# Paired PSUM banks, joined copies and sums, deferred activations and other attention places in a sketched attention and SwiGLU kernel

## The chip, the cores and the metric

The kernel runs on one core of a Trainium2 chip. The metric is the device time of one execution in microseconds; several executions are taken, and their median counts. Profiles are of one execution and give the span from the first to the last instruction.

## The reference

Four images (batches) of 1088 tokens with four heads of 32 go through a polynomial-sketch attention without softmax, and its output, 4352 tokens of 128, through a SwiGLU block with 1536 hidden channels. All is computed in float32.

```python
def phi(x):                                    # r = 8, so 64 features
    a = np.einsum('rd,bhsd->bhsr', S1, x)
    b = np.einsum('rd,bhsd->bhsr', S2, x)
    return np.einsum('bhsi,bhsj->bhsij', a, b).reshape(*x.shape[:-1], r * r)
q_p, k_p = (phi(q), phi(k))
kv = np.einsum('bhsf,bhsd->bhfd', k_p, v)
z = np.sum(k_p, axis=2)
num = np.einsum('bhsf,bhfd->bhsd', q_p, kv)
den = np.einsum('bhsf,bhf->bhs', q_p, z)[..., None] + 1e-06
attn = num / den
x = attn.transpose(0, 2, 1, 3).reshape(B * S, H * D)
g = x @ w_gate
out = (g * (1 / (1 + np.exp(-g))) * (x @ w_val)) @ w_out
```

## The kernel before

The tokens of each image are cut into three blocks of 384, 384 and 320 (`blocks`, numbers 0 to 11), the hidden channels into 12 chunks of 128. A unit is one block with one chunk: it makes the gate product and the value product of 128 channels by 384 or 320 tokens, the activation, and their product, the hidden tile. `down` then multiplies one hidden tile by 128 rows of `w_out` and adds it up in a PSUM bank over the 12 chunks of a block; after the twelfth, `store` transposes the bank on VectorE (DVE) and sends it out.

The program's order is the schedule: the engines work off their own queues in the order in which the code issues the instructions.

The first image's three blocks are worked in `unit` with whole float32 products, interleaved with the attention of images 0 and 1. From block 3 on a loop over y from 0 to 107 (units in the order of `line`) does the rest; the prediction numbers its units by y. There `cut_unit` makes a product out of three faster passes in place of one float32 product. Weights and tokens are split ahead of time into a high part, a scaled low part and a difference (`cut_weights`, `cut_tokens`: w1, wb, wd and x1, x0, xd). A first pass makes d = wd times xd, and two passes make p = w1 x1 + wb x0. ScalarE (ACT) copies d with a scale (L890), DVE adds p (L893), ACT takes the activation (L897) and GpSimd (POOL) multiplies activation and value to the hidden tile (L902). Up to y = 21 only the value product is made this way and the gate is a float32 product (L880); from y = 22 (`GATES`) both are. The gate's weights are split on the way, in rows of four steps each from y = 0, 1, 5 and 5 on (`gate_rows`, on ACT and DVE, L849).

PSUM has eight banks. Bank 3 holds the sums of `down` (`acc`). `bank()` hands out the one of the others that was touched longest ago; `wide("a")` is banks 4 and 5, `wide("b")` 6 and 7, which the attention uses. A unit with both products takes four single banks.

The attention of images 1 to 3 is a generator, `attentions()`. Each `yield` ends a part; the loop asks for parts (`parts_of`) after a unit: after each one up to y = 21, after every second one later. Large groups of TensorE work are marked `yield "pe"` and are placed before units 6, 8, 22, 24 and 40 (`GROUPS`). The first group of image b has the products of values and key features (`values`, L370), of the key sums (L698) and, for image 2, the key products of the next image (L336). `fold` and `spread_out` then take the results on DVE. The second has the query products (L324); the third, `numerators` (L760), ends in copies to `xT`. The key sums are five additions on POOL (`feature_sums`, L529); `beside` issues one of them with each part of the transpositions that follow. `query_step` begins with a chain of small DVE operations for the denominators (L727 to L733).

`todo` lists finished units; after each unit, one `down` is issued (two at times) when more than five are listed, or six where a new block begins.

Of the kernel before, what the change touches and what calls it, by code (L numbers as in the profile page):

```python
# [7 lines left out]
FP32 = mybir.dt.float32  # L8
# [4 lines left out]
AF = mybir.ActivationFunctionType  # L13
# [6 lines left out]
def kernel(  # L20
# [89 lines left out]
    def bank(tag=None):  # L110

        if tag is not None:
            i = place[tag]
        elif oldest[0]:
            i = min((i for i in used if i not in held), key=used.get)
        else:
            i = place[free_banks[turn[0] % len(free_banks)]]
            turn[0] += 1
        touch(i)
        return PS[:, i, :]  # L120

    def wide(tag):
        i = place[tag]
# [473 lines left out]
    def attentions():  # L597

        yield from turn_keys(1)
        yield from turn_queries(1)
        hold("a")
        kp = wide("a")
        for i, c in enumerate(kpieces):
            key_products(kp[:, i, :], *c)
        ka = apool.tile([P, NC * H, R], FP32, tag="kas", name="kas")

        def sketch(ps, i):
            c0, c1 = kpieces[i]  # L610
# [36 lines left out]

        phk = apool.tile([P, NC, H, R, R], FP32, tag="phk", name="phk")
        yield from features(phk, kab)
        zs, sums = feature_sums(phk)  # L650
        yield from beside(turn_keys(3), sums)
        yield from beside(turn_queries(2), sums)
        for b in (2, 3):
            yield "pe"
            if b == 3:
                numerators(2, spread)
            hold("a")
            kv = bank()
            release("a")
            values(kv, phk, zs)  # L660
            if b == 2:
                kab, copies = sketched(wide("a"), key_products, 2, "kab2")
                run_copies(copies, 2)
            fold(kv)
            spread = spread_out(b, kv)
            yield
            yield "pe"
            qab, copies = sketched(wide("b"), query_sketches, 3, "qab")
            run_copies(copies, 2)
            yield  # L670
# [112 lines left out]
    acc = {}  # L783
# [67 lines left out]
    def cut_tokens(i, engine=nc.gpsimd):  # L851
# [14 lines left out]
            op0=ALU.mult, op1=ALU.add,  # L866
        )

    def cut_unit(i, j, both=False):

        t0, n = blocks[i]
        x1, x0, xd = (x[:, 0:n] for x in x_parts[i])
        ws = (wg, wv) if both else (wv,)
        parts = [[x[:, j % 3, :] for x in w_parts[id(w), j // 3]] for w in ws]
        ds = [bank()[:, 0:n] for _ in ws]
        g = None if both else bank()[:, 0:n]
        for d, (_, _, wd) in zip(ds, parts):
            nc.tensor.matmul(d, wd, xd, start=True, stop=True)  # L878
        if not both:
            nc.tensor.matmul(g, wg[:, j, :], xT[:, t0 : t0 + n], start=True, stop=True)  # L880
        ps = []
        for w1, wb, _ in parts:
            p = bank()[:, 0:n]
            nc.tensor.matmul(p, w1, x1, start=True, stop=False)  # L884
            nc.tensor.matmul(p, wb, x0, start=False, stop=True)  # L885
            ps.append(p)
        sums = []
        for d in ds:
            s = fpool.tile([P, BW], FP32, tag="sgl", name="sum", bufs=6)[:, 0:n]
            nc.scalar.activation(s, d, AF.Copy, scale=-1.0 / BETA)  # L890
            sums.append(s)
        for p, s in zip(ps, sums):
            nc.vector.scalar_tensor_tensor(  # L893
                out=s, in0=p, scalar=1.0 + 1.0 / BETA, in1=s, op0=ALU.mult, op1=ALU.add
            )
        sg = fpool.tile([P, BW], FP32, tag="sg", name="sg", bufs=5)[:, 0:n]
        nc.scalar.activation(sg, sums[0] if both else g, AF.Silu)  # L897
        slot_of[i, j] = slots.pop(0)
        hj = hbuf[:, slot_of[i, j], :]
        hidden[i, j] = hj  # L900
        todo.append((i, j))
        nc.gpsimd.tensor_tensor(out=hj[:, 0:n], in0=sg, in1=sums[-1], op=ALU.mult)  # L902

    def unit(i, j, late=False, between=(None, None)):


        t0, n = blocks[i]
        g, u = bank(), bank()
        for o, w in ((g, wg), (u, wv)):
            if between[0] and w is wv:  # L910
                between[0]()
            nc.tensor.matmul(  # L912
                o[:, 0:n], w[:, j, :], xT[:, t0 : t0 + n], start=True, stop=True
            )
        sg = fpool.tile(
            [P, BW], FP32, tag="sgl" if late else "sg", name="sg", bufs=6 if late else 5
        )
# [14 lines left out]

    def catch_up():
        o, sg = lates.pop(0)
        nc.gpsimd.tensor_tensor(out=o, in0=o, in1=sg, op=ALU.mult)

    def down():

        i, j = todo.pop(0)
        n = SPLIT if i == LAST else blocks[i][1]  # L940
        if j == 0:
            acc[i] = bank("g1" if i == 1 else "acc")
        nc.tensor.matmul(  # L943
            acc[i][:, 0:n],
            wo[:, j, :],
# [199 lines left out]
    for z, (i, j) in enumerate(seq):  # L1145
# [16 lines left out]
        if z == 20:  # L1162
            lows = [
                pool.tile([P, 3, P], FP32, tag=tag, name="low", bufs=bufs)[:]
                for pool, tag, bufs in ((apool, "qb", 2), (apool, "dT", 2), (apool, "rd", 2), (fpool, "sgl", 6))
            ]
            first, low, second, third = cut_weights(wv, lows, nc.gpsimd)
        if z in (20, 21):
# [27 lines left out]

    line = [3 * b + k for b in range(1, B) for k in ((0, 2, 1) if b == B - 1 else range(3))]
    END = len(line) * NCH  # L1200
    GROUPS, GATES = (6, 8, 22, 24, 40), 22

    token_steps = {}
    for m, i in enumerate(line[1:], 1):
# [7 lines left out]
    for y in range(END):  # L1212
        i, j = line[y // NCH], y % NCH
        if y in GROUPS:
            group()
        if y == END - 1:
            unit(i, j)
        else:
            cut_unit(i, j, both=y >= GATES)
        for _ in range(2):  # L1220

            if len(todo) > min(5 + (todo[0][1] == 0), END - y + 1):
                down()
        parts_of(y < GATES or y % 2 == 0)
        if y == 0:
            gate_rows = cut_weights(wg, lows, nc.vector)
        for n, row in enumerate(gate_rows):
            if y >= (0, 1, 5, 5)[n]:
                take(row, 1)
        for gen in token_steps.get(y, ()):  # L1230
            next(gen, None)
# [43 lines left out]
```

## Time and profile before

| | us |
|---|---|
| median of 8 runs | 293.37 |
| lowest and highest | 291.91, 295.06 |
| the profiled execution | 293.55 |
| its span | 291.7 |
| loop over y, from its first product | 93.15 |
| last product of the loop's last unit ends about | 283.7 |

The mean granted TensorE clock is 0.994. The operations that the change touches, from the table of groups by shape (108 to 283 us):

| line, engine | columns | mean ns |
|---|---|---|
| L890 ACT copy of d | 384 / 320 | 485 / 430 |
| L893 DVE sum with p | 384 / 320 | 551 / 485 |
| L897 ACT activation of a sum | 384 / 320 | 526 / 472 |
| L902 POOL product | 384 / 320 | 1064 / 926 |

A float32 product stands in the trace as two matrix instructions, a pass of parts as one. The ends of matrix instructions are modelled, and one that waits for the engine before it shows a longer time; so starts are the safer numbers. The idle time that a row gives is that of its engine, and it costs something only where the engine is the one that sets the end.

### The profile page before, as it was taken

What the parts mean: (1) busy time and instruction counts of PE and PEld (TensorE: products, weight loads), DVE (VectorE), ACT (ScalarE), POOL (GpSimd) and SP (SyncE); (2) the same over time, 40 slices, a digit from 0 to 9 for tenths busy, and PEclk for the clock granted to TensorE, in tenths of its full rate; (3) what the DMA queues carried; (4) which work ended last, traced back from release to release, by engine and by line L of the source; (5) the groups of instructions that cost most, each with busy time, mean ns of one, the idle gap of its engine ahead of it and who ended that gap; (6) DMA issues with size and microseconds to landing.
All of it is one profiled execution on the core that took longest, in us unless ns stands there. A gap on an engine that the chain in (4) does not pass through costs nothing.

```text
span 291.7 us, 6382 instructions
## 1 busy us (share of the span) xinstructions
PE 282.4 (97%) x2307; PEld 213.7 (73%) x2307; DVE 206.5 (71%) x422; ACT 181.4 (62%) x432; POOL 162.6 (56%) x183
## 2 busy tenths in 40 slices
PE   8899999999999969999999999999999999999995
PEld 6545566656656657777787778888888988888984
DVE  3997988874667954999668876656767676676651
ACT  3467565732303826555467677788788887888860
POOL 3315322389301784589737666557666675766650
PEclk9999999999999979999999999999999999999999
DMA  7564293312410213001001001001001010010101
GB/s 193 153 215 110 58 288 100 104 51 83 108 21 15 52 57 88 0 1 27 7 12 27 2 0 24 2 0 31 0 0 27 2 24 1 2 27 0 23 2 27
DMA packets 26142, 14.33 MB, mean 49 GB/s; under 512 B 19840, under 2 KB 24192, under 8 KB 26112
## 3 DMA queue, kind: packets, MB, share of 16 engines
q1 hardware_dynamic: 25456, 13.84, 18.6%
q8 instruction: 18, 0.29, 0.4%
q10 hardware_dynamic: 656, 0.10, 0.2%
q14 instruction: 12, 0.10, 0.1%
HBM read 11.41 MB, written 2.23 MB: 47 GB/s over the span
## 4 chain that ended last, share of the span: by engine, by line
PE 86%; DVE 5%; POOL 3%; ACT 3%; issue 2%; DMA 2%; SPq 0%; DVEq 0%; POOLq 0%; ACTq 0%
PE PS L943 26%; PE PS L912 15%; PE PS L878 10%; PE PS L884 10%; PE PS L885 10%; PE PS L880 4%; PE PS L336 2%; PE PS L324 2%; PE PS L760 2%; POOL zs L529 2%; DMA kld<-in_k_dram 2%; ACT sum L890 1%; PE PS L370 1%; POOL hbuf L902 1%; DVE sum L893 1%
## 5 line engine op out<-in xcount | busy, mean ns | idle before, releaser
L902 POOL TENSOR_TENSOR hbuf<-sg,sum 128x384 f32<-128x384 f32 (+1 forms) x107 | 109.3, 1023 | 62.9 <-ACT sg L897 51.2
L893 DVE SCALAR_TENSOR_TENSOR sum<-PS,sum 128x384 f32<-128x384 f32 (+1 forms) x192 | 93.9, 526 | 50.2 <-ACT sum L890 42.1
L943 PE MATMUL PS<-hbuf,wo 128*128 128x384 f32 (+2 forms) x288 | 103.0, 459 | 0.0
L890 ACT ACTIVATE sum<-PS 128x384 f32<-128x384 f32 (+1 forms) x192 | 80.3, 464 | 13.5 <-PE PS L878 13.2
L897 ACT ACTIVATE sg<-sum 128x384 f32<-128x384 f32 (+1 forms) x85 | 42.7, 503 | 27.4 <-DVE sum L893 27.4
L943 PEld LDWEIGHTS PS<-hbuf,wo 128*128 128x128 f32 x288 | 52.0, 189 | 10.3 <-issue 0.4
L878 PE MATMUL PS<-xd,gphq 128*128 128x384 f32 (+1 forms) x85 | 47.9, 564 | 0.0
L884 PE MATMUL PS<-x,w 128*128 128x384 f32 (+1 forms) x107 | 42.2, 394 | 0.1
L878 PE MATMUL PS<-xd,wd 128*128 128x384 f32 (+1 forms) x107 | 39.7, 371 | 0.7 <-DVE sum L893 0.4
L885 PE MATMUL PS<-x,wb 128*128 128x384 f32 (+1 forms) x107 | 35.0, 327 | 0.0
L918 ACT ACTIVATE sg<-PS 128x384 f32<-128x384 f32 (+1 forms) x37 | 17.4, 473 | 22.0 <-PE PS L912 20.3
L912 PE MATMUL PS<-xT,wg 128*128 128x384 f32 (+1 forms) x74 | 29.5, 480 | 0.0
L912 PE MATMUL PS<-xT,wv 128*128 128x384 f32 (+1 forms) x74 | 28.8, 471 | 0.2 <-DVE wv L270 0.2
L878 PEld LDWEIGHTS PS<-xd,wd 128*128 128x128 f32 x107 | 20.4, 190 | 11.5 <-DVE sum L893 1.2
L884 PE MATMUL PS<-x,graw 128*128 128x384 f32 (+1 forms) x85 | 27.9, 328 | 0.0
L885 PE MATMUL PS<-x,graw 128*128 128x384 f32 (+1 forms) x85 | 27.6, 325 | 0.0
L929 DVE TENSOR_TENSOR hbuf<-sg,PS 128x384 f32<-128x384 f32 (+1 forms) x31 | 16.2, 526 | 10.8 <-PE PS L912 10.5
L884 PEld LDWEIGHTS PS<-x,w 128*128 128x128 f32 x107 | 20.1, 188 | 4.2 <-ACT sum L890 0.5
L878 PEld LDWEIGHTS PS<-xd,gphq 128*128 128x128 f32 x85 | 16.1, 189 | 8.6 <-issue 0.4
L885 PEld LDWEIGHTS PS<-x,wb 128*128 128x128 f32 x107 | 20.2, 188 | 2.9
L912 PEld LDWEIGHTS PS<-xT,wv 128*128 128x128 f32 x74 | 13.8, 190 | 9.2 <-DVE hbuf L929 0.9
L912 PEld LDWEIGHTS PS<-xT,wg 128*128 128x128 f32 x74 | 13.3, 189 | 9.3 <-issue 1.2
(130 smaller groups left out, 347.5 us busy)
## 6 DMA issues: line engine op xcount, KB each, us to landing
kld<-in_k_dram SPq DMA_DIRECT2D x4, 544.0 KB, 4.4
vld<-in_v_dram SPq DMA_DIRECT2D x12, 144.0 KB, 5.2
qld<-in_q_dram SPq DMA_DIRECT2D x3, 544.0 KB, 3.4
raw<-in_moe_w_out_dram SPq DMA_DIRECT2D x4, 384.0 KB, 4.6
out_dram<-o SPq DMA_DIRECT2D x28, 48.0 KB, 1.9
raw<-in_moe_w_gate_dram SPq DMA_DIRECT2D x3, 384.0 KB, 3.2
raw<-in_moe_w_val_dram SPq DMA_DIRECT2D x3, 384.0 KB, 3.3
out_dram<-o SPq DMA_DIRECT2D x16, 40.0 KB, 1.7
```

Of the source, the lines that this page charges most:

```text
L878: nc.tensor.matmul(d, wd, xd, start=True, stop=True)
L880: nc.tensor.matmul(g, wg[:, j, :], xT[:, t0 : t0 + n], start=True, stop=True)
L884: nc.tensor.matmul(p, w1, x1, start=True, stop=False)
L885: nc.tensor.matmul(p, wb, x0, start=False, stop=True)
L890: nc.scalar.activation(s, d, AF.Copy, scale=-1.0 / BETA)
L893: nc.vector.scalar_tensor_tensor(out=s, in0=p, scalar=1.0 + 1.0 / BETA, in1=s, op0=ALU.mult, op1=ALU.add)
L897: nc.scalar.activation(sg, sums[0] if both else g, AF.Silu)
L902: nc.gpsimd.tensor_tensor(out=hj[:, 0:n], in0=sg, in1=sums[-1], op=ALU.mult)
L912: nc.tensor.matmul(o[:, 0:n], w[:, j, :], xT[:, t0 : t0 + n], start=True, stop=True)
L918: nc.scalar.activation(sg[:, 0:n], g[:, 0:n], AF.Silu)
L929: nc.vector.tensor_tensor(out=hj[:, 0:n], in0=sg[:, 0:n], in1=u[:, 0:n], op=ALU.mult)
L943: nc.tensor.matmul(acc[i][:, 0:n], wo[:, j, :], hidden[i, j][:, 0:n], start=(j == 0), stop=(j == NCH - 1),)
```

## The change

What it does:

- The five key sums of image 2 are issued together, before the transpositions of the next keys and queries.
- A unit with both products takes two pairs of neighbouring banks (`pair`, out of banks 0-1, 4-5 and 6-7) in place of four single ones: one for both d, one for both p. ACT copies both d in one instruction of twice the size, and DVE makes both sums in one.
- In such a unit the activation and the POOL product are put off (`ending`) and issued by `finish` in the next unit, behind that unit's copy. The unit is listed for `down` then.
- Both products are made of parts from y = 26 on, and before that at y = 11, 14, 17, 20 and 23.
- The groups stand before y = 5, 7, 26, 28 and 52. Parts of the attention are asked for after each unit up to y = 7, after two of three up to 25, and after every third one from there.
- The rows of gate weights begin at y = 0, 2, 6 and 6.
- `acc` is bank 2 for every second block from block 5 on, and bank 2 is held back from y = 26. The rule with six listed units is left for one block alone.
- The buffers of the sums are four of two halves instead of six single ones; the fourth low part of the value weights has another home.

```diff
+    def pair():
+        i = min((i for i in (0, 4, 6) if i not in held), key=lambda i: max(used[i], used[i + 1]))
+        touch(i, i + 1)
+        return PS[:, i : i + 2, :]
...
         zs, sums = feature_sums(phk)
-        yield from beside(turn_keys(3), sums)
-        yield from beside(turn_queries(2), sums)
+        for f in sums:
+            f()
+        yield from turn_keys(3)
+        yield from turn_queries(2)
...
             kv = bank()
+            kv_bank = [max(used, key=used.get)]
...
             spread = spread_out(b, kv)
+            touch(*kv_bank)
...
+    room = [None, 2]
+    def doubles(k):
+        if room[1] + k > 2:
+            room[:] = fpool.tile([P, 2, BW], FP32, tag="sgl", name="sum", bufs=4), 0
+        at = room[1]
+        room[1] += k
+        return room[0][:, at : at + k, :]
...
-        ds = [bank()[:, 0:n] for _ in ws]
+        ds = pair()[:, :, 0:n] if both else bank()[:, 0:n].unsqueeze(1)
         g = None if both else bank()[:, 0:n]
...
-        ps = []
-        for w1, wb, _ in parts:
-            p = bank()[:, 0:n]
...
-        for d in ds:
-            s = fpool.tile([P, BW], FP32, tag="sgl", name="sum", bufs=6)[:, 0:n]
-            nc.scalar.activation(s, d, AF.Copy, scale=-1.0 / BETA)
...
-        for p, s in zip(ps, sums):
-            nc.vector.scalar_tensor_tensor(
-                out=s, in0=p, scalar=1.0 + 1.0 / BETA, in1=s, op0=ALU.mult, op1=ALU.add
-            )
...
+        sums = doubles(len(ws))[:, :, 0:n]
+        nc.scalar.activation(sums, ds, AF.Copy, scale=-1.0 / BETA)
+        finish()
+        ps = pair()[:, :, 0:n] if both else bank()[:, 0:n].unsqueeze(1)
+        for k, (w1, wb, _) in enumerate(parts):
+            nc.tensor.matmul(ps[:, k], w1, x1, start=True, stop=False)
+            nc.tensor.matmul(ps[:, k], wb, x0, start=False, stop=True)
+        nc.vector.scalar_tensor_tensor(
+            out=sums, in0=ps, scalar=1.0 + 1.0 / BETA, in1=sums, op0=ALU.mult, op1=ALU.add
+        )
+        def last():
+            sg = fpool.tile([P, BW], FP32, tag="sg", name="sg", bufs=5)[:, 0:n]
+            nc.scalar.activation(sg, sums[:, 0] if both else g, AF.Silu)
...
+            todo.append((i, j))
+            nc.gpsimd.tensor_tensor(out=hj[:, 0:n], in0=sg, in1=sums[:, len(ws) - 1], op=ALU.mult)
+        if both:
+            ending.append(last)
+        else:
+            last()
...
+    ending = []
+    def finish():
+        while ending:
+            ending.pop(0)()
...
-            acc[i] = bank("g1" if i == 1 else "acc")
+            acc[i] = bank("g1" if i == 1 else "g2" if i in line[2::2] else "acc")
...
-                for pool, tag, bufs in ((apool, "qb", 2), (apool, "dT", 2), (apool, "rd", 2), (fpool, "sgl", 6))
+                for pool, tag, bufs in ((apool, "qb", 2), (apool, "dT", 2), (apool, "rd", 2), (apool, "qb", 2))
...
-    GROUPS, GATES = (6, 8, 22, 24, 40), 22
+    GROUPS, GATES = (5, 7, 26, 28, 52), 26
...
+        if y == GATES:
+            hold("g2")
         if y == END - 1:
+            finish()
             unit(i, j)
         else:
-            cut_unit(i, j, both=y >= GATES)
+            cut_unit(i, j, both=y >= GATES or (y > 10 and y % 3 == 2))
         for _ in range(2):
-            if len(todo) > min(5 + (todo[0][1] == 0), END - y + 1):
+            if len(todo) > min(5 + (todo[0] == (line[1], 0)), END - y + 1):
                 down()
-        parts_of(y < GATES or y % 2 == 0)
+        parts_of(y < 8 or (y % 3 != 2 if y < GATES else y % 3 == 0))
...
-            if y >= (0, 1, 5, 5)[n]:
+            if y >= (0, 2, 6, 6)[n]:
                 take(row, 1)
```

More of the change, by code (lines that the diff above doesn't have):

```diff
@@ L874, in cut_unit @@
         parts = [[x[:, j % 3, :] for x in w_parts[id(w), j // 3]] for w in ws]
-        ds = [bank()[:, 0:n] for _ in ws]
+        ds = pair()[:, :, 0:n] if both else bank()[:, 0:n].unsqueeze(1)
         g = None if both else bank()[:, 0:n]
-        for d, (_, _, wd) in zip(ds, parts):
-            nc.tensor.matmul(d, wd, xd, start=True, stop=True)
+        for k, (_, _, wd) in enumerate(parts):
+            nc.tensor.matmul(ds[:, k], wd, xd, start=True, stop=True)
         if not both:
             nc.tensor.matmul(g, wg[:, j, :], xT[:, t0 : t0 + n], start=True, stop=True)
-        ps = []
@@ L882, in cut_unit @@
-        for w1, wb, _ in parts:
-            p = bank()[:, 0:n]
[L884 to L887, printed above, removed]
-        for d in ds:
-            s = fpool.tile([P, BW], FP32, tag="sgl", name="sum", bufs=6)[:, 0:n]
-            nc.scalar.activation(s, d, AF.Copy, scale=-1.0 / BETA)
-            sums.append(s)
-        for p, s in zip(ps, sums):
-            nc.vector.scalar_tensor_tensor(
-                out=s, in0=p, scalar=1.0 + 1.0 / BETA, in1=s, op0=ALU.mult, op1=ALU.add
-            )
@@ L896, in cut_unit @@
[L896 to L902, printed above, removed]
+        sums = doubles(len(ws))[:, :, 0:n]
+        nc.scalar.activation(sums, ds, AF.Copy, scale=-1.0 / BETA)
+        finish()
+        ps = pair()[:, :, 0:n] if both else bank()[:, 0:n].unsqueeze(1)
@@ new lines, in cut_unit @@
+        for k, (w1, wb, _) in enumerate(parts):
[7 more added lines that the diff above has]
+            nc.scalar.activation(sg, sums[:, 0] if both else g, AF.Silu)
+            slot_of[i, j] = slots.pop(0)
+            hj = hbuf[:, slot_of[i, j], :]
+            hidden[i, j] = hj
+            todo.append((i, j))
+            nc.gpsimd.tensor_tensor(out=hj[:, 0:n], in0=sg, in1=sums[:, len(ws) - 1], op=ALU.mult)
@@ L914, in unit @@
             )
-        sg = fpool.tile(
-            [P, BW], FP32, tag="sgl" if late else "sg", name="sg", bufs=6 if late else 5
-        )
+        sg = doubles(1)[:, 0, :] if late else fpool.tile([P, BW], FP32, tag="sg", name="sg", bufs=5)
         nc.scalar.activation(sg[:, 0:n], g[:, 0:n], AF.Silu)
@@ L935, in catch_up @@
         nc.gpsimd.tensor_tensor(out=o, in0=o, in1=sg, op=ALU.mult)
+    line = [3 * b + k for b in range(1, B) for k in ((0, 2, 1) if b == B - 1 else range(3))]
     def down():
@@ L1195 @@
     slots[:] = range(NH - 10)
-    line = [3 * b + k for b in range(1, B) for k in ((0, 2, 1) if b == B - 1 else range(3))]
     END = len(line) * NCH
-    GROUPS, GATES = (6, 8, 22, 24, 40), 22
+    GROUPS, GATES = (5, 7, 26, 28, 52), 26
     token_steps = {}
```

## The prediction

> **What bounds the kernel now.** I read the busy shares first, then the table of stretches, then the chain of waits between 96 and 110 us, then single queues.
>
> ```profile
> PE 282.4 (97%) x2307; PEld 213.7 (73%) x2307; DVE 206.5 (71%) x422; ACT 181.4 (62%) x432; POOL 162.6 (56%) x183
> ...
> 100.00:104.50 4.50, 2.19 (x77) 1.51 (x75) 4.50 (x8) 1.40 (x3) 4.42 (x5) 0.99 0.39 124
> 104.50:108.60 4.10, 4.08 (x49) 3.52 (x50) 1.27 (x5) 1.32 (x4) 4.10 (x4) 0.60 0.06 12
> ...
> 147.00:157.50 10.50, 10.39 (x64) 8.27 (x54) 7.92 (x18) 7.43 (x20) 5.68 (x7) 1.00 0.02 4
> 157.50:173.00 15.50, 15.36 (x78) 12.48 (x76) 13.08 (x26) 10.70 (x28) 9.44 (x10) 1.00 0.09 14
> 181.00:284.00 103.00, 103.00 (x523) 89.11 (x522) 66.92 (x140) 83.77 (x198) 66.46 (x69) 1.00 0.06 10
> ```
>
> In the stretches the columns are length, then busy PE, weight load, DVE, ACT, POOL, granted clock, DMA. From 181 to 284 us TensorE is never idle. Busy is not proof of peak, so I took the spacing of starts: unit after unit (six passes of 0.173 us and one output product of 0.646 us, sum 1.69) the output product starts at 239.76, 241.45, 243.14: 1.69 us apart. That stage has no slack; only TensorE work counts there. The hole is at 100 to 108.6: TensorE is idle for 2.3 us and then runs at a mean clock of 0.60.
>
> ```profile
> 96.41 0.97 POOL hbuf L902
> ...
> 97.39 1.28 POOL zs L529
> 98.67 0.94 POOL hbuf L902
> ...
> 99.91 1.28 POOL zs L529
> 101.19 1.28 POOL hbuf L902
> 102.47 1.00 POOL zs L529
> ...
> 103.55 0.93 POOL zs L529
> ...
> 104.52 0.44 PE PS L698 x8
> 104.97 2.12 PE PS L336 x36
> ```
>
> This chain (start, length, what) ends last there: the five key sums of image 2 stand on POOL between gate products (L902), because `beside` hands one out per step. The value product L698 waits for the last of them. After the wait the key products take 2.12 us; the same 36 took 1.20 at 57.01 and at 69.33. What the hole costs, from starts on TensorE: unit 5 waits 0.55 (99.06 to 99.61, for a bank that the sum of unit 2 on DVE frees); L698 waits 2.3, with 0.25 around it; the key products are 0.9 too long; unit 6 is 0.5 too long. Sum 4.5 us. The gaps from 139 to 177 us, as spacing above 0.173, 0.147, 0.646 or 0.54, come to about 3.7: 0.4 in the groups up to 147, 2.0 in gaps of 0.1 to 0.4 until 173, 1.3 around the last attention group at 173.35.
>
> **What the Trainium skill says.** "TensorE: Matmul & The Clock Gate", section "What's actually happening": after an idle window of about 3.4 us the matrix clock drops to half until it has been busy as long. The trace agrees in kind: 0.60 behind the hole, near 1.00 elsewhere; the hole itself is only 2.3 us, in a stretch that is half idle. "SBUF — State Buffer", section "SBUF: two separate sides": a DVE operation with two SBUF inputs and a GpSimd operation that reads SBUF exclude each other for the whole instruction. The trace fits it: the same 128x384 difference (L849 on DVE) takes 1.08, 1.50, 0.90 and 0.61 us beside POOL work. "Perfetto Trace Analysis", section "Optimizing Scalar/DVE Operations": each instruction carries a fixed access cost, so larger ones amortise it, but breaking up may help where a large one causes bubbles elsewhere. The rows agree on the fixed part: DVE's L893 takes 551 ns on 384 columns and 485 on 320, ACT's L890 485 and 430.
>
> **Part by part.**
>
> *Key sums in one go.* In the changed order all five sums stand ahead of the first gate product. First sum 92.70 to 94.13; the second waits for the last feature block (DVE, 94.68); then 1.28, 1.28, 1.03, 0.92: done at 99.2. The group moves from unit 6 to unit 5, so unit 4 (ends 99.06) is followed by the value products: 1.2 us, then L698 at 100.3. The sums are a microsecond early. The first bank of the group needs DVE's sum of unit 2, which now stands before the first weight difference, not behind it (gate rows begin at unit 2): transposes 0.8, 0.7, 0.8 and three sums of 0.5 from 95.03 end at 98.6. The key products need the bank of unit 3's sum for their second half, at 101.2; DVE has it at 101.0 if one difference takes 1.1, at 101.4 if 1.5. Key products 100.5 to 101.7, units 5 and 6 with one output product each to 105.3. The query group then wants the fold: differences at 1.0 each put it at 103.5 and its result at 104.3; with three of 1.5, nothing excludes that, at 106. So after these units and two output products TensorE stands at 105.3, where before it stood at 109.94 (unit 7's true start). Gain 4.6; bounds 3.3 (all three differences 1.5, waits of 0.2 and 0.9 put in) and 4.7. With no hole the clock stays up; that is in these numbers. Delayed gate products: unit 0's moves from 96.41 to 99.2, but its first reader is an output product at about 102.9. I take 4.3.
>
> *Units with both products in parts.* Before, units 22 to 106: 85. After, 26 to 106 and 11, 14, 17, 20, 23: 86. One more exchange of 0.646 for three passes of 0.173: gain 0.13.
>
> *Joined copies and sums.* By the two sizes, ACT's copy costs 155 ns plus 0.86 a column: joined 0.82 for 2x384 and 0.71 for 2x320, in place of 0.97 and 0.86. DVE's sum is 155 plus 1.03: 0.95 and 0.81. 86 units save some 13 us on each engine, but beside TensorE at its peak this is worth nothing by itself. The price is a later first result. Worst case, 320-wide unit of 1.42 us (0.88 plus a 320 output product): both ds products end at 0.29, copy 0.5 to 1.2 (0.2 from product to copy, as 240.58 to 240.78), sum 1.25 to 2.07. Three pairs rotate: ds of unit y+2 takes the pair of unit y's sum at 2.83 (slack 0.76); ps of unit y+1 takes the pair of unit y's copy at 1.71 (slack 0.5). The activation of unit y now stands behind copy y+1, so ACT no longer waits for DVE first; its result is read by an output product six units later instead of five. ACT load 0.71+0.47 of 1.42. So nothing is added as long as DVE is free.
>
> *DVE not free.* In units 26 to 52 attention parts come every third unit, each near 1.0 us: sum y+1 then ends at 3.9 of 4.25, no wait. The chain of denominators (148.90 to 150.94, 2.04 us) stands behind sum 30: sum 31 ends at 4.95, ds of unit 33 wanted it at 4.25: wait 0.7. At the group of unit 26 no output product lies between unit 26 and 27, because the deferred unit adds nothing to the list; unit 27's pair holds bank 1, which fold and transposition read for 1.0 us after the value products (142.04 to 143.41 before, 1.4): wait 0.4 to 0.9. The query group needs the pair of sum 27: wait 0.5. One copy behind the query copies: 0.2. Sum about 2.0; against 2.4 before (0.4 + 2.0). At unit 52 the numerators need sum 51 (0.6) and unit 52's second pair the copy out of bank 4 (0.7): 1.3, as before. Bounds: none of these waits but the last, gain 2.4, to twice them, loss 1.6. I take a gain of 0.4.
>
> *Mixed stage, units 11 to 25.* Three units take 5.3 us (units 1.17, 1.17, 1.04, three output products); DVE has two sums of 0.55, one of 0.95 and two parts near 1.0. The chain of denominators at unit 15 delays sum 17 to 7.6 us after its start; its bank is wanted at 7.8. I take 0; up to 1 if it slips.
>
> *Output banks.* Alternating banks 2 and 3 remove the extra unit of delay at a block change; the trace shows no wait there (two products together at 237.58 and 256.71). 0. The fourth weight tile moves to another buffer, read last at 28 us: 0.
>
> *End.* One more output product is left behind the last line (1.2 us of its products, 0.86, behind it instead of 1.7), so the last transposition, its DMAs and those of the last copy lie closer together: plus 0.2; 0 to 0.6.
>
> Sum: -4.3 - 0.1 - 0.4 + 0.2 = -4.6. The profiled execution took 293.55 (span 291.7 and 1.85 around it): 288.95. It lies 0.2 above the median of 293.37, so I forecast 288.9.
>
> **Rivals.** 0.5% is 1.5 us, about what a measurement of this kernel tells from no change.
> - *Likeliest, 0.55*: as summed, 287.4 to 290.4.
> - *The waits of units 26 to 52 go as well, 0.12*: 4.6 + (2.4 - 0.4) = 6.6, so 286.9. For it: DVE is busy only 7.9 of 10.5 us there. Against: the chain of denominators is one block of 2 us.
> - *DVE takes POOL's place in the hole, 0.15*: differences of 1.5 against back-to-back gate products, the fold late, and half clock again: gain 3.3, less 0.9 for the clock, less the other lines at nothing: about 291. For it: 1.50 at 100.10. Against: two others took 0.9 and 0.61.
> - *The pairs bind, slower, 0.12*: three pairs where single banks freed half by half. It decides once the way from ds to the end of the sum passes 2.83 us in a 320 unit (2.07 by my count), or copy plus reach passes 1.71. A two-bank access dearer by 0.45 on each of ACT and DVE does that; then each of some 81 units loses about 0.1, 8 us, less 4.3: 297. Against: two-bank copies of xT take 589 (ACT, 512 columns) and 692 ns (DVE), no dearer than one-bank rates.
> - *Gain and new waits cancel, 0.06*: 293.
>
> Faster by over 0.5%: 0.55 + 0.12 + 0.13 = 0.80; within 0.08; slower 0.12. The range 286.5 to 292.3 holds all but the slower cases and a few per cent.
>
> **What would show it.** Right: the five sums adjoin on POOL from 92.7 to about 99.3, L698 starts near 100.3 without a wait on POOL, the key products take 1.2, the clock stays near 1.00 from 100 to 110; the joined sums take about 0.95 and 0.81. Wrong in the middle: more than 1 us of waits on DVE's sum at units 33 or 27. Wrong in the large: unit spacing in the last 100 us above 1.69 (384) or 1.42 (320), then the pairs bind.

## The result

| kernel | median us (range) | ratio to before [95%] | span of the profiled execution |
|---|---|---|---|
| before | 293.38 (291.85 to 295.06, 31 runs) | | 291.7 |
| after | 289.76 (289.38 to 290.98, 11 runs) | 0.9887 [0.9865, 0.9909] | 288.3 |

The gain is 3.6 us at the median; the forecast was 288.9, a gain of 4.5. Part of that gain is the end of a loss of clock that the kernel before has only in some of its executions, described in the last section: 12 of the 31 took 291.85 to 292.50 us, the other 19 took 293.23 or more, and against the median of the 12 (292.09) the gain is 2.3 us. The start of the program is not the same in all profiles, so what follows it is compared on a clock of its own: "the loop" below runs from the first product of unit 0 with `xd` to the end of the span. It took 198.6 us before and 194.9 after: 3.7 less.

The profile after, first the busy shares on its page:

```profile
PE 279.2 (97%) x2308; PEld 212.2 (74%) x2308; DVE 205.8 (71%) x337; ACT 173.4 (60%) x347; POOL 162.5 (56%) x183
```

DVE and ACT issue 85 instructions fewer each, the joined sums and copies. TensorE's busy time fell by 3.2 us, though it has the same products but for one exchange; 1.4 us of that, by the prediction's reading, is what key products and a unit had lost at half clock. Next the stretches (columns as in the prediction):

```profile
100.00:104.50 4.50, 4.50 (x103) 3.66 (x91) 4.43 (x10) 2.21 (x6) 4.50 (x5) 1.00 0.39 124
104.50:108.60 4.10, 4.10 (x82) 3.02 (x81) 2.29 (x4) 2.58 (x7) 4.10 (x4) 1.00 0.11 22
...
155.00:171.00 16.00, 14.71 (x78) 12.65 (x77) 13.95 (x18) 11.65 (x21) 9.23 (x11) 1.00 0.07 11
180.00:280.00 100.00, 99.75 (x559) 84.73 (x558) 63.24 (x73) 73.62 (x130) 62.97 (x67) 1.00 0.06 10
```

The hole of 100 to 108.6 us is closed: TensorE is busy throughout, at a mean clock of 1.00 where it was 0.60. The last hundred microseconds are nearly as full as before (99.75 of 100 against 100.00; the rest is one wait of 0.24 at unit 52), and the output products there start 1.69 us apart as before (173.43, 175.12, 176.81). A new hole stands between 155 and 171 us: 1.3 us in which TensorE is idle, against 0.25 in that stretch before.

POOL's queue at the key sums (start, length, engine, line, operation; in brackets the idle time ahead and what ended it):

```profile
92.98 1.43 POOL L535 TENSOR_TENSOR zs<-phk 128x512 f32<-128x512 f32 x1 [14.15 <-DVE phk L365]
95.03 1.28 POOL L535 TENSOR_TENSOR zs<-phk 128x512 f32<-128x512 f32 x1 [0.63 <-DVE phk L365]
96.40 2.11 POOL L535 TENSOR_TENSOR zs<-zs 128x512 f32<-128x512 f32 x2
98.59 0.74 POOL L535 TENSOR_TENSOR zs<-zs,phk 128x256 f32<-128x256 f32 x1
99.28 4.85 POOL L919 TENSOR_TENSOR hbuf<-sg,sum 128x384 f32<-128x384 f32 x4
```

And TensorE's own queue there:

```profile
99.42 1.21 PE L376 MATMUL PS<-phk,vld 128*32 128x64 f32 x72
100.45 0.29 PE L708 MATMUL PS<-zs,ones 128*32 128x64 f32 x8
100.68 1.27 PE L342 MATMUL PS<-s,kT 128*64 128x64 f32 x36
```

The sums are over at 99.33, 1.1 us before L708 (L698 of before) uses them. It starts without a wait, and the key products take 1.27 us, not 2.19. What TensorE waits for in the rest of the loop stands in its waits (engine, waiting line, what it waited for: us, times, longest):

```profile
PE PS L898 <- DVE sum L908: 1.3, 1, 1.3
...
PE PS L330 <- DVE sum L908: 0.5, 1, 0.5
PE PS L898 <- DVE gphq L859: 0.4, 1, 0.4
```

All three are waits for DVE. The first is at unit 33, the second at the query group behind unit 27, the third before unit 11. By the starts on TensorE, which include the slower first product after a wait, they cost 1.55, 0.64 and 0.72 us. The timeline of unit 33:

```profile
154.77 0.85 DVE L737 TENSOR_TENSOR dot<-qab 128x288 f32<-128x288 f32 x1
...
155.66 0.45 DVE L740 TENSOR_REDUCE den<-dot 128x36 f32<-128x288 f32 x1
...
156.15 0.60 DVE L741 TENSOR_SCALAR den<-den 128x36 f32<-128x36 f32 x1
...
156.78 0.38 DVE L742 RECIPROCAL den<-den 128x36 f32<-128x36 f32 x1
157.20 0.46 DVE L743 TENSOR_TENSOR qab<-qab,den 128x288 f32<-128x288 f32 x1
157.57 1.55 DVE L908 SCALAR_TENSOR_TENSOR sum<-PS,sum 128x640 f32<-128x640 f32 x2
...
158.44 0.42 PE L898 MATMUL PS<-xd,gphq 128*128 128x320 f32 x1 [1.29 <-DVE sum L908]
```

The chain of denominators holds DVE from 154.77 to 157.57, then comes a joined sum, and only when that whole sum is done has unit 33 a pair of banks.

### The profile page after: what moved, and what is told of

It is laid out like the page before. It is cut to its first block, busy times and chain, and to the rows that moved or that the text cites. A ratio compares the mean times of both kernels' runs of the same rounds, so it can differ in the third digit from the quotient of the medians.

```text
span 288.3 us, 6035 instructions
## 1 busy us (share of the span) xinstructions
PE 279.2 (97%) x2308; PEld 212.2 (74%) x2308; DVE 205.8 (71%) x337; ACT 173.4 (60%) x347; POOL 162.5 (56%) x183
## 4 chain that ended last, share of the span: by engine, by line
PE 88%; DVE 6%; DMA 2%; ACT 1%; issue 1%; SPq 0%; DVEq 0%; ACTq 0%
PE PS L972 26%; PE PS L941 16%; PE PS L898 11%; PE PS L906 10%; PE PS L907 10%; PE PS L900 4%; PE PS L770 2%; PE PS L342 2%; PE PS L330 2%; DMA kld<-in_k_dram 2%; PE PS L376 2%; DVE sum L908 1%; PE PS L987 1%; DVE gphq L859 1%; PE PS L485 1%
## 5 line engine op out<-in xcount | busy, mean ns | idle before, releaser
L919 POOL TENSOR_TENSOR hbuf<-sg,sum 128x384 f32<-128x384 f32 (+1 forms) x107 | 107.7, 1012 | 58.9 <-ACT sg L914 54.6
L908 DVE SCALAR_TENSOR_TENSOR sum<-PS,sum 128x768 f32<-128x768 f32 (+3 forms) x107 | 88.6, 830 | 46.7 <-ACT sum L902 40.9
L902 ACT ACTIVATE sum<-PS 128x768 f32<-128x768 f32 (+3 forms) x107 | 76.5, 715 | 43.7 <-PE PS L898 39.9
L898 PE MATMUL PS<-xd,gphq 128*128 128x384 f32 (+1 forms) x86 | 49.6, 577 | 1.7 <-DVE sum L908 1.3
L906 PE MATMUL PS<-x,w 128*128 128x384 f32 (+1 forms) x107 | 41.0, 383 | 0.0
L898 PE MATMUL PS<-xd,wd 128*128 128x384 f32 (+1 forms) x107 | 38.2, 357 | 0.2 <-DVE xd L874 0.2
L906 PE MATMUL PS<-x,graw 128*128 128x384 f32 (+1 forms) x86 | 28.1, 327 | 0.2 <-ACT xT L787 0.2
L907 PE MATMUL PS<-x,graw 128*128 128x384 f32 (+1 forms) x86 | 28.0, 326 | 0.0
L945 ACT ACTIVATE sg<-PS 128x384 f32<-128x384 f32 (+1 forms) x31 | 14.4, 467 | 21.3 <-PE PS L941 19.6
```

Of the source, the lines that this page charges most:

```text
L898: nc.tensor.matmul(ds[:, k], wd, xd, start=True, stop=True)
L902: nc.scalar.activation(sums, ds, AF.Copy, scale=-1.0 / BETA)
L906: nc.tensor.matmul(ps[:, k], w1, x1, start=True, stop=False)
L907: nc.tensor.matmul(ps[:, k], wb, x0, start=False, stop=True)
L908: nc.vector.scalar_tensor_tensor(out=sums, in0=ps, scalar=1.0 + 1.0 / BETA, in1=sums, op0=ALU.mult, op1=ALU.add)
L919: nc.gpsimd.tensor_tensor(out=hj[:, 0:n], in0=sg, in1=sums[:, len(ws) - 1], op=ALU.mult)
```

## The experiments

All of them compute the whole reference. The ratios are against runs of the kernel before on the same chip, whose medians lay between 293.38 and 293.49; "loop" is from the one profiled execution. In before, e1 and e8 the query group stands one unit later, behind unit 7 instead of 6, so 1.82 us of its time there are that unit and its output product.

| kernel | median us | ratio to before [95%] | loop us | query group, us into the loop |
|---|---|---|---|---|
| before | 293.38 | | 198.6 | 18.70 |
| after | 289.76 | 0.9887 [0.9865, 0.9909] | 194.9 | 12.29 |
| e1_sums_only | 291.05 | 0.9934 [0.9911, 0.9957] | 196.1 | 16.23 |
| e2_sums_spread | 296.45 | 1.0116 [1.0088, 1.0143] | 200.5 | 17.94 |
| e8_groups_6_8 | 291.26 | 0.9939 [0.9914, 0.9965] | 196.4 | 15.39 |
| e9_sums_and_groups | 289.97 | 0.9888 [0.9854, 0.9923] | 195.1 | 13.68 |
| e3_single_banks | 289.89 | 0.9890 [0.9863, 0.9917] | 195.0 | 13.48 |
| e12_single_touch | 288.99 | 0.9858 [0.9836, 0.9881] | 194.0 | 12.27 |
| e4_no_deferral | 336.98 | 1.1499 [1.1467, 1.1530] | 242.2 | 12.28 |
| e5_chain_halved | 288.62 | 0.9856 [0.9820, 0.9892] | 193.8 | 12.28 |
| e6_first_at_14 | 288.51 | 0.9843 [0.9811, 0.9875] | 193.8 | 12.28 |
| e10_rows_early | 288.87 | 0.9852 [0.9823, 0.9881] | 194.3 | 12.45 |
| e7_three | 287.33 | 0.9803 [0.9775, 0.9831] | 192.7 | 12.28 |
| e11_rows_chain_banks | 287.58 | 0.9806 [0.9765, 0.9847] | 192.7 | 12.46 |

### The front: sums and groups

**The sums alone**, in the kernel before (e1):

```diff
-        yield from beside(turn_keys(3), sums)
-        yield from beside(turn_queries(2), sums)
+        for f in sums:
+            f()
+        yield from turn_keys(3)
+        yield from turn_queries(2)
```

> The kernel before, with only the five key sums of image 2 issued together. Theory (the order on POOL makes the hole): the sums end near 99.3 us, the value product of the key sums before unit 6 waits for nothing, the key products behind it take 1.2 us instead of 2.1, the clock stays near 1.00. Unit 5's wait of 0.55 stays. Gain 2.3 + 0.25 + 0.9 + 0.5, about 3.9 us: 289.4. Rival 1 (the earlier groups and the joined work give the gain): less than 1 us, above 292.4. Rival 2 (DVE takes POOL's place): a new wait of 1 us or more at the same group, 291 to 292.

The loop is 2.5 us shorter, not the 3.9 expected: the second rival came. TensorE's queue in e1, its first product of sums and its key products:

```profile
102.89 0.29 PE L700 MATMUL PS<-zs,ones 128*32 128x64 f32 x8
105.03 1.27 PE L336 MATMUL PS<-s,kT 128*64 128x64 f32 x36 [1.85 <-DVE sum L895]
```

and DVE's queue in e1 before it:

```profile
102.34 0.90 DVE L851 TENSOR_TENSOR hbuf<-wg,graw 128x384 f32<-128x384 f32 x1
103.17 0.54 DVE L895 SCALAR_TENSOR_TENSOR sum<-PS,sum 128x384 f32<-128x384 f32 x1
103.63 0.88 DVE L851 TENSOR_TENSOR hbuf<-wg,graw 128x384 f32<-128x384 f32 x1
104.44 0.54 DVE L895 SCALAR_TENSOR_TENSOR sum<-PS,sum 128x384 f32<-128x384 f32 x1
```

POOL is out of the way: L700 has no wait. But the key products then wait 1.85 us for a bank, until DVE has the sum of unit 5, which ends at 104.98 behind the weight differences. In the kernel before this second wait lay in the shadow of POOL's; whoever removes only the wait that ended last finds the next one behind it.

**The sums spread again**, in the kernel after (e2): the same lines reversed.

> The changed kernel with the key sums handed out again one per part. Theory: the last sum ends near 104.5 us as before, but the group now stands a unit earlier, so TensorE waits some 4 us for it instead of 2.3 and runs at half clock after it: 4.5 to 6 us slower than the changed kernel, 294 to 296, slower than before. Rival (other parts of the change fill the hole): within 1 us of the changed kernel, below 291.

The loop is 5.6 us longer than after, longer even than before. TensorE's queue in e2:

```profile
105.59 0.44 PE L706 MATMUL PS<-zs,ones 128*32 128x64 f32 x8 [3.95 <-POOL zs L535]
105.96 2.19 PE L342 MATMUL PS<-s,kT 128*64 128x64 f32 x36
```

With the group a unit earlier and the sums no earlier, the wait for POOL grows from 2.33 to 3.95 us, and the half clock returns: 2.19 us for the key products. So moving the groups pays only together with the sums.

**The groups at 6 and 8**, in the kernel after (e8):

```diff
-    GROUPS, GATES = (5, 7, 26, 28, 52), 26
+    GROUPS, GATES = (6, 8, 26, 28, 52), 26
```

> The changed kernel with its first two groups before units 6 and 8 again. Theory (the order of the sums, not the place of the group, gives the gain): within 0.4 us of the changed kernel, 289.4 to 290.2. Rival (the earlier place is part of the gain, since unit 5 waits for a bank before): 0.5 us or more slower.

```profile
103.50 1.27 PE L342 MATMUL PS<-s,kT 128*64 128x64 f32 x36 [1.23 <-DVE sum L908]
```

This line of e8's TensorE queue shows the wait of e1 again, 1.23 us long here. The loop is 1.46 us longer than after, so the rival came and not the theory: that is what the place of the group is worth. Before unit 5 its key products need the sum of unit 3 instead of that of unit 5.

**Sums and groups alone**, in the kernel before (e9): the diff of e1 and

```diff
-    GROUPS, GATES = (6, 8, 22, 24, 40), 22
+    GROUPS, GATES = (5, 7, 22, 24, 40), 22
```

> The kernel before with the sums together and its first two groups before units 5 and 7; gate rows, later groups, units and parts as before. Theory (the group before unit 6 finds bank 4 just taken by unit 5, whose sum DVE makes last; before unit 5 it needs only unit 3's): the wait of 1.85 us that the sums alone left at the key products is mostly gone; what is left there, 0.5 to 1.3 us, is DVE being one weight difference behind. 1 to 1.5 us faster than the sums alone: 289.6 to 290.1. Rival (the place does not matter): 291.

It is as fast as the whole change (289.97 against 289.76): the sums and the first two groups alone give its gain. It has a wait that the kernel after hasn't; TensorE's queue in e9:

```profile
104.19 0.91 PE L882 MATMUL PS<-xT,wg 128*128 128x384 f32 x2 [0.96 <-DVE spread L710]
```

The gate product of unit 6 drew the bank from which DVE was still reading `kv` into `spread`. The kernel after marks this bank as just used again, with the two lines `kv_bank = ...` and `touch(*kv_bank)` of the diff, so that the rotation gives it out last. What those two lines are worth at this place, e12 below measures.

### The joined copies and sums

**All of it but the pairs** (e3): the kernel before with the sums together, the groups, the units in parts, the rate of attention parts and the gate rows of the kernel after, on single banks, with single copies and sums and nothing put off. The bank of `down`, the rule of its list and the buffers are those of before too, and the two lines on `kv`'s bank are missing.

```diff
-    GROUPS, GATES = (6, 8, 22, 24, 40), 22
+    GROUPS, GATES = (5, 7, 26, 28, 52), 26
...
-            cut_unit(i, j, both=y >= GATES)
+            cut_unit(i, j, both=y >= GATES or (y > 10 and y % 3 == 2))
...
-        parts_of(y < GATES or y % 2 == 0)
+        parts_of(y < 8 or (y % 3 != 2 if y < GATES else y % 3 == 0))
...
-            if y >= (0, 1, 5, 5)[n]:
+            if y >= (0, 2, 6, 6)[n]:
```

> The kernel before with the sums together, the groups, the mixed gates, the part rate and the gate rows of the changed kernel, but its own units: single banks, two copies, two sums, the activation at once, one output bank. Theory (TensorE sets the pace, so the joined work is worth nothing by itself): within 1 us of the changed kernel, 288.8 to 290.8. It is possibly faster, where the wider steps of the pairs made the waits at units 27, 28 and 33 longer. Rival (the joined copies and sums carry part of the gain): 292 or more, with gaps between units behind every attention part.

No difference from after at the median (289.89), and in its loop it pays 0.83 us, by starts, for the same wait as e9, which TensorE's queue in e3 shows:

```profile
104.08 0.91 PE L882 MATMUL PS<-xT,wg 128*128 128x384 f32 x2 [0.66 <-DVE spread L710]
```

**e3 with the two lines on that bank** (e12):

```diff
             kv = bank()
+            kv_bank = [max(used, key=used.get)]
...
             spread = spread_out(b, kv)
+            touch(*kv_bank)
```

> The single-bank units of the earlier run, with the one line of the change added that marks the value bank as just used after the fold. Theory (unit 6 waited 0.83 us because its gate product drew the bank that the fold still read): that wait goes, 289.1, so the joined and deferred work of the change is worth nothing or costs up to 0.7 us. Rival (the wait moves to another bank, and pairs are worth what it costs): 289.6 or more, level with the changed kernel.

The wait is gone, and the loop is 1.0 us shorter than e3's and 0.9 shorter than after's. The intervals of after and e12 overlap, so at the median the 0.8 us between them is not established; the trace says where it lies. In e12's stretches:

```profile
155.00:171.00 16.00, 16.00 (x86) 13.89 (x85) 12.94 (x29) 11.77 (x30) 9.45 (x11) 1.00 0.08 13
```

TensorE is full where the kernel after is idle for 1.3 us. Two things differ there. A unit on single banks can begin on the first bank that comes free, where a pair comes free with the whole joined sum of 0.82 us. And the chain of denominators takes 2.04 us in e12 and e3, but 2.80 in the kernel after; two of its operations in e12:

```profile
156.75 0.45 DVE L731 TENSOR_TENSOR dot<-qab 128x288 f32<-128x288 f32 x1
...
157.72 0.25 DVE L735 TENSOR_SCALAR den<-den 128x36 f32<-128x36 f32 x1
```

No run separates the two. So joining, pairing and putting off give nothing here, and by the trace take back somewhat under a microsecond, a part of it through the longer chain; the second bank of `down` and the rule of its list, which e12 lacks too, were not measured alone.

**Nothing put off** (e4), in the kernel after:

```diff
-        if both:
-            ending.append(last)
-        else:
-            last()
+        last()
```

> The changed kernel with the activation issued in its own unit, joined copies and pairs kept. Theory (the deferral is what lets the joined steps be free): ACT does copy, waits for the whole joined sum on DVE, does the activation, and only then the next copy, so a unit cannot be shorter than 0.71 + 0.82 + 0.46 + 0.1 = 2.1 us (320 columns) or 0.81 + 0.95 + 0.51 + 0.1 = 2.4 us (384), against 1.42 to 1.69: about 0.65 us for each of 81 units, 50 us, near 340. Rival (ACT's order does not matter, as TensorE sets the pace): within 2 us of the changed kernel.

47 us slower than after. ACT and DVE in e4's timeline:

```profile
251.18 0.79 ACT L902 ACTIVATE sum<-PS 128x768 f32<-128x768 f32 x1
...
252.01 0.96 DVE L908 SCALAR_TENSOR_TENSOR sum<-PS,sum 128x768 f32<-128x768 f32 x1 [1.24 <-ACT sum L902]
...
253.00 0.52 ACT L914 ACTIVATE sg<-sum 128x384 f32<-128x384 f32 x1 [1.03 <-DVE sum L908]
...
253.43 0.79 ACT L902 ACTIVATE sum<-PS 128x768 f32<-128x768 f32 x1
```

A ring: copy, sum, activation, and only then the next copy, since the activation stands ahead of it in ACT's queue and waits for DVE. One turn takes 2.25 us (251.18 to 253.43), where TensorE has 1.58 us of work (six passes of 0.173 and an output product of 0.54). Putting the activation off is therefore no gain of its own, but without it this joining costs 47 us.

### The middle

**The chain of denominators in two parts** (e5), in the kernel after, the second part asked for behind unit 31:

```diff
         nc.vector.tensor_reduce(out=den[:], in_=dot[:], axis=AX.X, op=ALU.add)
+        if b == 3:
+            yield
...
-        parts_of(y < 8 or (y % 3 != 2 if y < GATES else y % 3 == 0))
+        parts_of(y < 8 or (y % 3 != 2 if y < GATES else y % 3 == 0 or y == 31))
```

> The changed kernel with image 3's chain of denominators cut in two: product and reduction behind unit 30, the other three behind unit 31. Theory (the chain stands as one block in front of sum 31, whose pair unit 33 wants): no wait of TensorE over 0.3 us at unit 33 in place of 1.45, 1.3 to 1.6 us faster than the changed kernel: 288.3. Rival (the wait is only put off, DVE is short of time there as a whole): the wait turns up at units 34 to 37 and the time stays within 0.5 us of the changed kernel.

**Unit 11 not in parts** (e6), in the kernel after:

```diff
-            cut_unit(i, j, both=y >= GATES or (y > 10 and y % 3 == 2))
+            cut_unit(i, j, both=y >= GATES or (y > 11 and y % 3 == 2))
```

> The changed kernel without the gate in parts at unit 11; units 14, 17, 20, 23 keep it. Theory (unit 11 waits for the last difference of the gate weights, which DVE makes only then): the wait of 0.6 us in front of unit 11 goes, 0.13 us of TensorE work comes back: 0.4 to 0.6 us faster, 289.3. Rival (DVE is late for another reason): a like wait at unit 12 to 14, no gain.

**Both, and another pair for the query group** (e7): e5, e6 and

```diff
-            qab, copies = sketched(wide("b"), query_sketches, 3, "qab")
+            qab, copies = sketched(wide("b" if b == 2 else "a"), query_sketches, 3, "qab")
```

> The two edits above together, and image 3's query products in banks 4 and 5 in place of 6 and 7, which the sum of unit 27 still holds. Theory: 1.4 + 0.5 + 0.6 = 2.5 us faster than the changed kernel: 287.3. Rival (the waits follow each other and only the longest counts): 288.3 or more.

How full TensorE is from 105 to 175 us, in the stretches of after, e5, e6 and e7, in this order:

```profile
105.00:175.00 70.00, 67.79 (x569) 52.91 (x568) 55.47 (x79) 44.88 (x86) 50.05 (x47) 1.00 0.09 19
```

```profile
105.00:175.00 70.00, 69.04 (x574) 53.97 (x574) 55.38 (x80) 45.55 (x87) 50.88 (x47) 1.00 0.10 20
```

```profile
105.00:175.00 70.00, 68.68 (x573) 53.75 (x572) 55.84 (x80) 45.36 (x88) 49.86 (x47) 1.00 0.10 20
```

```profile
105.00:175.00 70.00, 69.94 (x579) 54.89 (x579) 55.08 (x80) 46.28 (x88) 50.71 (x48) 1.00 0.10 20
```

The idle time falls from 2.21 us to 0.96, 1.32 and 0.06. In the loop e5 gains 1.09 us on after (1.3 to 1.6 were expected; by the starts, 0.3 us of the wait stays at unit 33), e6 1.12, and e7 2.21: their sum. So nothing is left for the third edit of e7 to add. e6 did more than it was made for: besides the wait before unit 11 the one of 0.64 us at the query group is gone too. With unit 11 off the pairs, the rotation has shifted: followed through the code, banks 6 and 7, which the query group uses, then hold the sum of unit 26 last, and not that of unit 27. e7 is the fastest kernel of the study, about 6 us faster than before, and its interval lies wholly under that of after.

**The gate rows at their old places** (e10), in the kernel after:

```diff
-            if y >= (0, 2, 6, 6)[n]:
+            if y >= (0, 1, 5, 5)[n]:
```

> The changed kernel with the gate rows from units 0, 1, 5 and 5 on. Theory: the gap of 0.6 us before unit 11 goes, since its weights are made a unit earlier, but the sums of units 2 and 3 stand behind one difference more when the value and key products want their banks: 0.5 to 1.2 us of wait there. Together within 0.6 us of the changed kernel, 289.2 to 290.4. Rival (the later rows carry part of the gain): slower by 1 us or more; rival (they only cost): faster by 0.6.

The loop is 0.57 us shorter than after's. The wait before unit 11 is gone, since the last difference of the gate weights is made earlier, and at the front nothing came in its place: the query group starts 12.45 us into the loop against 12.29. The rival that they only cost came: the later rows, which the prediction had counted as a help for the group's first bank, cost more than they give.

**e10, e5 and the other pair together** (e11):

> The changed kernel with the chain in two halves, image 3's query products in banks 4 and 5, and the gate rows from units 0, 1, 5 and 5 on with unit 11 made of parts again. Theory (the waits of 1.45, 0.6 and 0.6 us are separate and add up): 0.1 to 0.3 us faster than the three edits with unit 11 left out, by the one product in parts: 287.1. Rival (a row that comes earlier costs elsewhere once the other waits are gone): 287.6 or more.

The loop is 192.7 us, as long as e7's and not 0.1 to 0.3 shorter: the wait before unit 11 can be taken away by either edit, and that of the query group by either shift of the pairs.

## Why the prediction was right, and where its steps were off

The right case was taken, and its sum was a microsecond too large. (Its last line slips by 0.1: 288.95 less the 0.2 by which the profiled execution lies above the median is 288.75, not 288.9.) By its own steps, on the loop:

| step | predicted | measured | from |
|---|---|---|---|
| front | -4.3 (walked 4.6, bounds 3.3 to 4.7) | -4.6 | query group 18.70 to 12.29 us into the loop, less one unit with its output product (1.82) |
| one more unit in parts | -0.13 | not measured alone | |
| mixed stage, units 11 to 25 | 0, up to 1 | +0.7 | the gap before unit 11 |
| units 26 to 52 | -0.4 | +0.2 | 1.55 + 0.64 + 1.2 at the numerators and the unit behind them + 0.5 in small gaps = 3.9, against the 3.7 that the prediction read |
| output banks, value tile | 0 | not measured alone | |
| end | +0.2 | +0.1 | start of the last product of `straight` to the end, 3.93 us against 3.85 |
| sum | -4.6 | -3.7 | 198.6 to 194.9 us |

**The front.** The number held: L708 at 100.45 (100.3), the sums over at 99.33 (99.2 to 99.3), key products of 1.27 (1.2), the clock at 1.00. The differences on DVE took 1.38, 0.89, 0.89 and 0.77 us and no wait came of them, so the rival that DVE takes POOL's place is out for the whole change; where the group stays before unit 6 it comes true (e1, e8). What the forecast's opening had put forward as the cause, the wait for POOL, is only a part: e1 gains 2.5 of the 4.6. The prediction did walk the banks and saw that the group needs the sums of units 2 and 3, but it did not ask what the sums alone would leave; e1 and e8 show a wait of 1.85 and 1.23 us there. Nor did it price the two lines on `kv`'s bank, without which the front gives back 0.8 (e3) to 1.1 us (e9) in a wait. The parts of the front are not additive: e2 is slower than before, with the group moved and the sums left spread. And there was some luck: the 1.4 us at half clock were counted as always there, while the kernel before loses them in about two of three executions; its median is one of those.

**Joined copies and sums.** Priced at nothing, and nothing came of them (e3, e12). Their lengths were right, as the groups by shape of after show:

```profile
L908 DVE SCALAR_TENSOR_TENSOR sum<-PS,sum 128x768 f32<-128x768 f32 x52 | 49.6, 954 | 24.9 <-ACT sum L902 23.5 <-ACT sg L914 1.1 <-PE PS L898 0.3
L902 ACT ACTIVATE sum<-PS 128x768 f32<-128x768 f32 x52 | 42.3, 813 | 23.5 <-PE PS L898 21.3 <-issue 1.0 <-POOL hbuf L919 0.9
L908 DVE SCALAR_TENSOR_TENSOR sum<-PS,sum 128x640 f32<-128x640 f32 x34 | 27.9, 823 | 17.4 <-ACT sum L902 17.4
...
L902 ACT ACTIVATE sum<-PS 128x640 f32<-128x640 f32 x34 | 24.0, 706 | 13.1 <-PE PS L898 12.1 <-POOL x L870 0.9
```

954 and 823 ns against 0.95 and 0.81, 813 and 706 against 0.82 and 0.71: reading two neighbouring banks in one instruction costs at most 0.01 us beyond the rate of one bank. With these the slack of the pairs holds in the steady stage, and the slower rival is out: the spacing of 1.69 us stands unchanged. That a late result can bind is real all the same, though not through the pairs: in e4 it is the order of ACT's queue, for 47 us.

**Where it was off: the middle.** The term of unit 33 was named at the right place with the right cause, but too small: 0.7 against 1.55. The chain of denominators was put at the 2.04 us that it took before; here it took 2.80, which accounts for 0.76 of the missing 0.85. `dot` took 0.85 us in place of 0.45 and the scalar addition 0.60 in place of 0.25. Each met a POOL product that had begun before it (154.43 to 155.31, 155.84 to 156.72): `dot` ended 0.31 us behind the first, the addition 0.03 behind the second. It is the same in the other profiles: beside a POOL product that is already running, `dot` ends 0.31 to 0.33 us behind it and the addition 0.03 to 0.06; with none running at its start, `dot` takes 0.41 to 0.45 and the addition 0.17 or 0.18. The kernel before had shown both cases, at image 2 and at image 3, and the prediction took the second for a constant:

```profile
124.58 0.71 DVE L727 TENSOR_TENSOR dot<-qab 128x288 f32<-128x288 f32 x1
...
125.82 0.39 DVE L731 TENSOR_SCALAR den<-den 128x36 f32<-128x36 f32 x1
...
148.90 0.45 DVE L727 TENSOR_TENSOR dot<-qab 128x288 f32<-128x288 f32 x1
...
149.88 0.25 DVE L731 TENSOR_SCALAR den<-den 128x36 f32<-128x36 f32 x1
```

The Trainium skill has the rule ("SBUF — State Buffer", section "SBUF: two separate sides"), which the prediction used for the differences, but not here: a DVE operation with two SBUF inputs and a GpSimd operation that reads SBUF shut each other out for the whole instruction. `dot` has two such inputs. The scalar addition has one, for which the page asks for a two-port mode; no run here shows in which mode it ran, only that it too waits for POOL. In e7, with POOL idle, it takes 0.17 us:

```profile
154.98 0.17 DVE L743 TENSOR_SCALAR den<-den 128x36 f32<-128x36 f32 x1
```

The second miss is the mixed stage: put at 0, it cost 0.7, not by the denominators that the prediction feared there but by the last difference of gate weights. Unit 11, the first that makes its gate product of parts, needs it at 114.7, and DVE ends it at 115.25, since its row was moved from y = 5 to y = 6 (e10):

```profile
114.23 1.02 DVE L859 SCALAR_TENSOR_TENSOR gphq<-hbuf,graw 128x384 fp32r<-128x384 f32 x1
...
115.30 0.44 PE L898 MATMUL PS<-xd,gphq 128*128 128x384 f32 x1 [0.45 <-DVE gphq L859]
```

The prediction looked at the moved rows only for what they free in front, not for who reads them last. The waits at the query group (0.64 against 0.5) and at the numerators (1.2 against 1.3) were right; that of unit 27, put at 0.4 to 0.9, came to about 0.25, by the starts.

## What to carry to other kernels

Behind the wait that ends last there is often a second one a little shorter: before pricing a repair at the whole hole, walk the other inputs of the waiting instruction as if the first were there (here POOL's sums, then DVE's sum for the bank, then the bank that `kv` is still read from). A moved producer is to be checked at its last reader as well as at its first, and a chain of small DVE operations is to be priced with the POOL products that will lie beside it. Joining two reads of PSUM banks into one saves instruction time, but it frees its banks in one piece; where the engine is not the bound, as here, the saving bought nothing.

## What the runs showed of the hardware

**The same program loses its clock in some executions and not in others.** With the runs of the kernel before that were made beside the experiments, the mean granted clock is on record for each execution. The 18 with a clock of 1.00 took 291.80 to 292.77 us (median 292.10), 37 with 0.988 or 0.994 took 293.32 to 295.68 (median 293.58), and one more, with 0.986, took 296.50. The difference of 1.5 us is about what the prediction read as lost at half clock behind the hole (0.9 and 0.5). The change takes the loss away: all 11 executions of the kernel after were granted 0.998 to 1.000.

In the profiles, before lost its clock on a wait of 2.33 us and e2 on one of 3.95 us, but e1 waited 1.85 us at the same place and its key products ran at full speed (1.27 us); of e1's 14 executions one, at 0.994, shows a loss, and of e2's four all do (0.988 or 0.994). Taking the lost clock as half, the time at half speed was about the same in both losses: 3.3 us before, from a mean clock of 0.60 over 4.1 us, which is (1 - 0.60) x 2 x 4.1; 3.4 us in e2, from 0.86 and 0.80 over two stretches of 5 us. The second figure agrees with the windows of about 3.4 us in "TensorE: Matmul & The Clock Gate", section "What's actually happening", of the Trainium skill; a loss after a wait of only 2.33 us does not agree with a whole idle window. That one program does both speaks against the length of the wait as what decides alone; but only one execution of each kernel has a trace, so whether it is the place of the wait in a window stays open.

**The start of the program is not the same each time.** The first image's key products took 1.49 to 1.53 us in most profiles and 2.19 in those of e1, e2 and e12, where the loop began about a microsecond later (94.4 to 94.5 us into the span against 92.8 to 93.4). That is as large as several of the effects studied here, and the reason why loops are compared and not spans.

**Which banks come next is a state that every unit changes.** e6 changed one unit at 115 us and with it took away a wait of 0.64 us at 148 us.
